# Gated mix of attention and a channel MLP: weight fetches, gate and row-max pacing moved in a kernel bound by one matmul stream

## The chip, the cores and the metric

The kernel runs on one core of one Trainium2 chip. The metric is device time of one execution in microseconds (us). TensorE (PE) multiplies, VectorE (DVE), ScalarE (ACT) and GpSimd (POOL) do the rest, and SyncE (SP) issues most transfers.

## The reference

```python
B, S, D, H, F = 1, 2048, 448, 16, 1792          # Dh = 28
g = sigmoid((x * gate_w).sum(-1, keepdims=True))
qkv = (x @ wqkv) split into q, k, v of 16 heads
p = softmax(q @ k^T * Dh ** -0.5)                # 2048 x 2048 for each head
a = (p @ v, heads joined) @ wo
y = layernorm(x)
b = gelu(y @ w1 + b1) @ w2 + b2
out = g * a + (1 - g) * b
```

All inputs and the output are float32. The kernel keeps accuracy with a split: each operand is a rounded high part (`h`, written by ScalarE or VectorE in the type fp32r) and a low part (`l`, value minus high part), and a product is h·h + h·l + l·h.

## The kernel before, in words

Tokens are worked on in 4 chunks (`NC`) of 512 (`CH`), heads in 4 groups (`NG`) of 4, one head to each 32-row strip of TensorE's array. TensorE's order is written out by hand for the whole kernel. In the first stage a scheduler orders the other engines; from the MLP on their order is by hand too. Each engine, and SP's queue, works strictly in its order.

**Stage 1, q, k and v (`qk_tile`, `v_tile`).** For each chunk `c` there are 7 tiles `m` of q and k columns and 4 tiles of v. In chunk 0, `load_wqk(m)` fetches a tile of weights into `wraw` (L147, 2 buffers), ScalarE makes the high part, GpSimd the low part. Results are copied out of the 8 PSUM banks in turn and written to DRAM by SP (L183). Between the tiles stand the steps of LayerNorm: `stats_fetch` and `ln_stats` (row statistics from `xk`), `ln_rows` and `ln_turn` (mean and reciprocal deviation, turned by TensorE with `ident` and written to DRAM), `ln_load` (read back to all partitions), `ln_fetch` and `ln_apply` (normalised x, on GpSimd). The first MLP weights (`fetch_w1`, `split_w1`) end the stage.

**Stage 2, the MLP.** For each chunk, `mlp1(f)` makes 14 tiles of 128 hidden units with 11 matmuls each (L512), and `mlp2(c, i)` makes 4 tiles of 128 tokens with 42 matmuls each (L525, L526, L529). I call them first and second product. In chunk 0 the weights are fetched and split as the tiles go: `split_w1` high part on ScalarE (L101), low part on GpSimd (L102), `split_w2` high part on ScalarE, low part on VectorE (L111). GpSimd also makes the low part of each hidden tile (L517).

**Row maxima beside it.** Attention needs the maximum of each row of scores first. `RowMax` computes q·k again, one unit being a 128 x 512 block (L346) in a PSUM bank which VectorE reduces (L326 one bank, L328 two). There are 16 groups of 65 units, 1040 in all; a group closes with a last reduction (L362), a TensorE transpose, a copy (L315) and a write. In the MLP `Filler` spreads the first 476 (`MLP_MAX`) over the matmuls: after each matmul `filler.run(n)` adds `n` to a slot count, and when six units are due by the share of slots passed, six are issued into banks 2 to 7.

```python
due = self.first + (self.upto - self.first) * min(1, self.slot / self.slots) - self.done
```

Before, each matmul counts 1; pacing begins at tile `FS` = 4 of chunk 0. A matmul into a bank whose reduction is not done waits, and everything behind it on TensorE too.

**The gate.** After the last chunk's first products ScalarE takes an exponential of `zall` (L572), and VectorE makes `gate` and `ngate` of it (L573 to L575). They are used in the last quarter of attention.

**Stage 3, attention.** 256 steps of 128 keys, with four score units each. `scores` takes five units at a time: three products per unit (L466), exponentials by ScalarE (L471), up to three row-max units, and then the products with v (L708). `load_wo(g)` in the first steps fetches a quarter of the output weights into one of 2 buffers `ob` (L685), VectorE copies the high part (L686), GpSimd makes the low part (L687). They are used from the last head group on.

Of the kernel before, what the change touches and what calls it, by code (L numbers as in the profile page):

```python
# [15 lines left out]
P = 128  # L16
S = 2048
D = 448
# [15 lines left out]
FS = 4  # L34
LQ = 12
# [4 lines left out]
def kernel(ctx: ExitStack, tc: tile.TileContext, xt, wqk, wv, wo, xk, w1, b1, w2, b2,  # L40
# [26 lines left out]
    nc.sync.dma_start(ones, one_t)  # L67
# [29 lines left out]
    def split_w1(f):  # L97
        r = wraw.pop((1, f)).rearrange("p (t x) -> p t x", t=4)
        t = mw1.tile([P, 8, P], F32R, name=f"w1f{f}")
        w1h[f], w1l[f] = t[:, 0:4], t[:, 4:8]  # L100
        nc.scalar.activation(w1h[f], r, AF.Copy)  # L101
        nc.gpsimd.tensor_sub(w1l[f], r, w1h[f].bitcast(F32))  # L102
# [33 lines left out]
    with tc.tile_pool(name="qx", bufs=2) as qx, tc.tile_pool(name="qo", bufs=3) as qo, \  # L136
# [9 lines left out]
        def load_wqk(m):  # L146
            raw = qx.tile([P, 4, P], F32, name="wraw", bufs=2)  # L147
            nc.sync.dma_start(raw, wqk[m])
            wh[m] = qw.tile([P, 4, P], F32R, name=f"wh{m}")
            wl[m] = qw.tile([P, 4, P], F32R, name=f"wl{m}")  # L150
            nc.scalar.activation(wh[m], raw, AF.Copy)
            nc.gpsimd.tensor_sub(wl[m], raw, wh[m].bitcast(F32))
# [81 lines left out]
        for t in range(4):  # L234
            load_x(0, t)
        for c in range(NC):
            for m in range(NM):
                if c == 0:
                    if m + 1 < NM:
                        load_wqk(m + 1)  # L240
                    if m == 1:
                        for t, s in ((ident, ident_d), (sel, sel_d), (b1s, b1)):
                            nc.sync.dma_start(t, s)
# [18 lines left out]
                if c == 1 and m >= 3 or c == 2 and m < 2:  # L262
                    stats_fetch(m - 1 if c == 1 else m + 6)
                if c == 1 and m >= 5 or c == 2 and m < 4:
                    ln_stats(m - 3 if c == 1 else m + 4)
                if c == 2 and m == 1:
                    ln_load(0)
                if c == 2 and m in (2, 3, 5, 6):
                    ln_fetch(0, (2, 3, 5, 6).index(m))
                if c == 2 and m in (4, 5) or c == 3 and m in (0, 1):  # L270
                    ln_apply(0, m - 4 if c == 2 else m + 2)
# [4 lines left out]
                if c == 3 and m == 1:  # L276
                    stages += [lnr[:, 0], lnr[:, 1]]
                if c == 3 and m in (1, 2, 4):
                    fetch_w1(m // 2 if m < 4 else 2) if m > 1 else fetch_w1(0)
# [224 lines left out]
    def mlp1(f):  # L504
# [6 lines left out]
        for i, (a, b) in enumerate(ops):  # L511
            nc.tensor.matmul(ps, a, b, start=(i == 0), stop=(i == len(ops) - 1))  # L512
            filler.run(1)
# [5 lines left out]
    def mlp2(c, i):  # L519
# [4 lines left out]
        for f in range(NF):  # L524
            nc.tensor.matmul(a, hh[f][:, sl], w2h[f], start=(f == 0), stop=False)  # L525
            nc.tensor.matmul(a, hh[f][:, sl], w2l[f], start=False, stop=False)  # L526
            if not last:
                filler.run(2)
            nc.tensor.matmul(a, hl[f][:, sl], w2h[f], start=False, stop=(f == NF - 1))  # L529
            if not last:  # L530
                filler.run(1)
# [7 lines left out]
    with tc.manual_schedule(engines={E.SP, E.Pool, E.Activation, E.DVE}):  # L539
        for c in range(NC):  # L540
            for f in range(NF):
                if c == 0:
# [7 lines left out]
                    if f == FS:  # L550
                        filler.spread(nc.sync, MLP_MAX, (NC * NF - FS) * 23 - 3 * NF)
                mlp1(f)
                if c == 0:
                    if f + 2 < NF:
                        split_w1(f + 2)
# [5 lines left out]
            if c == NC - 1:  # L561
# [9 lines left out]

                nc.scalar.activation(gate, zall, AF.Exp, scale=-1.0)  # L572
                nc.vector.tensor_scalar_add(gate, gate, 1.0)  # L573
                nc.vector.reciprocal(gate, gate)
                nc.vector.tensor_scalar(ngate, gate, -1.0, 1.0, op0=OP.mult, op1=OP.add)  # L575
# [9 lines left out]
            for i in range(TPC):  # L585
                mlp2(c, i)
                if c + 1 < NC and i < 3:
# [95 lines left out]
    def load_wo(g):  # L683
        worw = ao.tile([P, D], F32, name="ob")
        nc.sync.dma_start(worw, wo[:, g])  # L685
        nc.vector.tensor_copy(woh[:, g], worw)  # L686
        nc.gpsimd.tensor_sub(wol[:, g], worw, woh[:, g].bitcast(F32))  # L687
# [25 lines left out]
    with tc.manual_schedule(engines={E.SP, E.Pool, E.Activation, E.DVE}):  # L713
# [5 lines left out]
        for u in range(0, 4 * steps, U):  # L719
            units = list(range(u, min(u + U, 4 * steps)))  # L720
            while at < units[-1] // 4:
# [3 lines left out]
                if n == 0:  # L725
# [3 lines left out]
                    if 2 <= k < 6:  # L729
                        load_wo(k - 2)  # L730
# [88 lines left out]
```

## Time and profile before

| | us |
|---|---|
| median of 3 runs | 1157.71 (1154.74 to 1160.45) |
| profiled execution, time | 1159.02 |
| profiled execution, span of the core | 1157.2 |
| TensorE busy | 1127.3 |
| VectorE busy | 734.4 |
| ScalarE busy | 634.7 |
| GpSimd busy | 334.2 |

Times within the profile count from the start of the span. A line `L512` is line 512 of the kernel before. The mean granted TensorE clock of the execution is 0.988. In the busy rows a matmul's bar lasts longer than the distance to the next one, since matmuls are pipelined: what a matmul costs is read from start to start. Where the profile names who ended a wait for several signals, it names the one that came last.

### The profile page before, as it was taken

What the parts mean: (1) busy time and instruction counts of PE and PEld (TensorE: products, weight loads), DVE (VectorE), ACT (ScalarE), POOL (GpSimd) and SP (SyncE); (2) the same over time, 40 slices, a digit from 0 to 9 for tenths busy, and PEclk for the clock granted to TensorE, in tenths of its full rate; (3) what the DMA queues carried; (4) which work ended last, traced back from release to release, by engine and by line L of the source; (5) the groups of instructions that cost most, each with busy time, mean ns of one, the idle gap of its engine ahead of it and who ended that gap; (6) DMA issues with size and microseconds to landing.
All of it is one profiled execution on the core that took longest, in us unless ns stands there. A gap on an engine that the chain in (4) does not pass through costs nothing.

```text
span 1157.2 us, 19820 instructions
## 1 busy us (share of the span) xinstructions
PE 1127.3 (97%) x8136; PEld 681.4 (59%) x8136; DVE 734.4 (63%) x1031; ACT 634.7 (55%) x668; POOL 334.2 (29%) x355
## 2 busy tenths in 40 slices
PE   6999999999999999979999999999999999999998
PEld 4888667777767766834444444444444444454556
DVE  3443298888888987356666766676666766656102
ACT  5333550241131132157887878787887877756463
POOL 4033563343333341021223121310223024425050
PEclk9999999999999998989999999999999999999899
DMA  8888542010110105072101211112021003011101
GB/s 264 255 259 295 171 126 79 17 45 26 61 49 18 42 9 126 17 178 69 29 12 35 57 52 24 35 28 50 19 63 35 18 19 90 12 47 53 57 27 48
DMA packets 53519, 84.35 MB, mean 73 GB/s; under 512 B 8676, under 2 KB 28660, under 8 KB 52628
## 3 DMA queue, kind: packets, MB, share of 16 engines
q1 hardware_dynamic: 49236, 76.96, 22.0%
q0 software_dynamic: 4192, 6.12, 2.1%
q8 instruction: 64, 1.05, 0.4%
q14 instruction: 27, 0.22, 0.1%
HBM read 56.40 MB, written 26.49 MB: 72 GB/s over the span
## 4 chain that ended last, share of the span: by engine, by line
PE 89%; DVE 4%; DMA 2%; issue 2%; POOL 1%; ACT 1%; SPq 0%; DVEq 0%; POOLq 0%
PE bank L708 21%; PE bank L466 20%; PE bank L346 15%; PE bank L512 10%; PE bank L179 6%; PE bank L529 4%; PE bank L525 4%; PE bank L526 4%; DVE mx L328 3%; PE bank L195 2%; PE bank L618 1%; PE bank L619 1%; PE bank L620 1%; DMA lt<-ob 1%; DMA wraw<-in_wqk 0%
## 5 line engine op out<-in xcount | busy, mean ns | idle before, releaser
L471 ACT ACTIVATE pt<-bank 128x1536 f32<-128x1536 f32 (+1 forms) x408 | 482.4, 1234 | 166.7 <-PE bank L466 166.7
L326 DVE TENSOR_REDUCE mx<-bank 128x1 f32<-128x512 f32 x624 | 412.9, 686 | 167.6 <-PE bank L346 153.8
L708 PE MATMUL bank<-pt,vg 128*32 128x512 f32 x2038 | 263.5, 607 | 0.0
L328 DVE TENSOR_REDUCE mx<-bank 128x2 f32<-128x1024 f32 x200 | 234.8, 1217 | 32.9 <-PE bank L346 32.9
L346 PE MATMUL bank<-khi,qd 28*128 28x512 f32 x512 | 241.8, 480 | 1.9 <-DVE mx L326 1.9
L346 PEld LDWEIGHTS bank<-khi,qd 28*128 28x128 f32 x512 | 92.4, 181 | 150.1 <-DVE mx L326 109.5
L466 PE MATMUL bank<-qh,klo 28*128 28x512 f32 x1024 | 180.0, 397 | 0.0
L466 PE MATMUL bank<-qh,khi 29*128 29x512 f32 x768 | 162.1, 484 | 0.0
L512 PE MATMUL bank<-y,w1f 128*128 128x512 f32 x616 | 153.5, 399 | 3.0 <-POOL w1f L102 2.6
L512 PEld LDWEIGHTS bank<-y,w1f 128*128 128x128 f32 x616 | 112.2, 188 | 39.9 <-issue 11.3
L466 PE MATMUL bank<-ql,khi 28*128 28x512 f32 x768 | 134.4, 394 | 0.0
L517 POOL TENSOR_TENSOR hl<-h,hh 128x512 fp32r<-128x512 f32 x56 | 73.3, 1309 | 136.2 <-ACT h L516 95.4
L346 PE MATMUL bank<-khr,qd 28*128 28x512 f32 x512 | 86.5, 473 | 10.7 <-DMA ql<-qk 5.8
L708 PEld LDWEIGHTS bank<-pt,vg 128*32 128x32 f32 x2038 | 45.7, 108 | 84.6 <-issue 83.7
L466 PEld LDWEIGHTS bank<-qh,klo 28*128 28x128 f32 x1024 | 91.0, 187 | 4.3
L515 ACT ACTIVATE hh<-bank,b1s 128x512 fp32r<-128x512 f32 x56 | 38.6, 689 | 99.6 <-PE bank L512 99.6
L634 POOL DMA_DIRECT2D lt<-ob x15 | 10.9, 724 | 277.6 <-DVE ob L633 277.6
L535 ACT ACTIVATE h<-bank 128x448 f32<-128x448 f32 x16 | 8.7, 546 | 149.1 <-PE bank L529 113.8
L529 PE MATMUL bank<-w2h,hl 128*128 128x448 f32 x224 | 85.7, 383 | 0.0
L525 PE MATMUL bank<-w2h,hh 128*128 128x448 f32 x224 | 84.8, 379 | 0.0
L466 PEld LDWEIGHTS bank<-qh,khi 29*128 29x128 f32 x768 | 63.4, 183 | 36.0 <-ACT pt L471 31.8
L526 PE MATMUL bank<-w2l,hh 128*128 128x448 f32 x224 | 82.9, 370 | 0.0
(110 smaller groups left out, 1256.6 us busy)
## 6 DMA issues: line engine op xcount, KB each, us to landing
qk<-hl SPq DMA_DIRECT2D x28, 512.0 KB
xraw<-in_xt SPq DMA_DIRECT2D x16, 256.0 KB
vs<-vt SPq DMA_DIRECT2D x16, 256.0 KB
s<-in_xt SPq DMA_DIRECT2D x16, 256.0 KB
rc<-rls POOLq DMA_DIRECT2D x60, 64.0 KB, 2.2
bxr<-in_xk SPq DMA_DIRECT2D x8, 448.0 KB
gbs<-h SPq DMA_DIRECT2D x16, 224.0 KB
klo<-qk SPq DMA_DIRECT2D x16, 224.0 KB
```

Source lines behind the costliest of these rows:

```text
L179: nc.tensor.matmul(ps, a, b, start=(i == 0), stop=(i == len(ops) - 1))
L326: nc.vector.reduce_max(self.mx[:, c0:c0 + 1], bank[:, b0], axis=AX)
L328: nc.vector.reduce_max(self.mx[:, c0:c1 + 1:c1 - c0], bank[:, b0:b1 + 1], axis=AX)
L346: nc.tensor.matmul(bank[:, b], self.qds[self.n][r, i * P:(i + 1) * P], khi[self.n // NC][r, k * 512:(k + 1) * 512], start=True, stop=True)
L466: nc.tensor.matmul(bank[:, u % U], a[r, k * P:(k + 1) * P], b[r], start=(i == 0), stop=(i == 2))
L471: nc.scalar.activation(t, bank[:, b:b + len(units)], AF.Exp, scale=SCALE)
L512: nc.tensor.matmul(ps, a, b, start=(i == 0), stop=(i == len(ops) - 1))
L517: nc.gpsimd.tensor_sub(hl[f], h, hh[f].bitcast(F32))
L525: nc.tensor.matmul(a, hh[f][:, sl], w2h[f], start=(f == 0), stop=False)
L526: nc.tensor.matmul(a, hh[f][:, sl], w2l[f], start=False, stop=False)
L529: nc.tensor.matmul(a, hl[f][:, sl], w2h[f], start=False, stop=(f == NF - 1))
L708: nc.tensor.matmul(pv[32 * j:32 * j + 32, :], vg[n // NC][:, k, 32 * j:32 * j + 32], probs.pop(4 * step + j), start=(k == 0), stop=(k == N ...
```

## The change

- The tiles `wraw` get 4 buffers instead of 2, and weights are fetched two tiles ahead instead of one. The constants `ident`, `sel`, `b1s` and the write of `ones` move from the start to chunk 1. The LayerNorm steps stand at other tiles.
- The low parts of w1 tiles 0 to 5 are made by VectorE instead of GpSimd.
- A slot of the row-max pacing counts 0.233 for a first-product matmul (0.8 of that in chunk 0) and 0.205 for a second-product matmul, instead of 1. The total of slots changes with it.
- VectorE's three gate operations stand after the first tile of the last chunk's second product.
- Output weights are fetched in two pairs at steps 2 and 7, and split at steps 7 and 12, instead of one at each of steps 2 to 5, fetch and split together.

```diff
+W1, W2 = 0.233, 0.205
-    nc.sync.dma_start(ones, one_t)
...
-    def split_w1(f):
+    def split_w1(f, lo):
...
-        nc.gpsimd.tensor_sub(w1l[f], r, w1h[f].bitcast(F32))
+        lo.tensor_sub(w1l[f], r, w1h[f].bitcast(F32))
...
-            raw = qx.tile([P, 4, P], F32, name="wraw", bufs=2)
+            raw = qx.tile([P, 4, P], F32, name="wraw", bufs=4)
...
+        load_wqk(1)
...
-                    if m + 1 < NM:
-                        load_wqk(m + 1)
+                    if m + 2 < NM:
+                        load_wqk(m + 2)
...
-                if c == 0 and m in (3, 5):
-                    stats_fetch(m // 4)
-                if c == 1 and m in (1, 2):
-                    ln_stats(m - 1)
-                if c == 1 and m == 3:
+                if c == 1 and m >= 2 or c == 2 and m < 3:
+                    ln_stats(m - 2 if c == 1 else m + 5)
+                if c == 1 or c == 2 and m == 0:
+                    stats_fetch(m if c == 1 else 7)
+                if c == 1 and m == 1:
+                    for t, d in ((ident, ident_d), (sel, sel_d), (b1s, b1), (ones, one_t)):
+                        nc.sync.dma_start(t, d)
+                if c == 1 and m == 4:
                     ln_rows(0, TPC)
-                if c == 1 and m == 6:
+                if c == 2 and m == 0:
                     ln_turn(0, TPC)
...
-                if c == 2 and m == 1:
+                if c == 2 and m == 2:
                     ln_load(0)
...
-                    split_w1(m - 4)
+                    split_w1(m - 4, nc.vector)
...
-            filler.run(1)
+            filler.run(W1 if c else 0.8 * W1)
...
-                filler.run(2)
+                filler.run(2 * W2)
...
-                filler.run(1)
+                filler.run(W2)
...
-                        filler.spread(nc.sync, MLP_MAX, (NC * NF - FS) * 23 - 3 * NF)
+                        filler.spread(nc.sync, MLP_MAX, 11 * W1 * (0.8 * (NF - FS) + 3 * NF) + 3 * W2 * NF * (NT - 1))
...
-                        split_w1(f + 2)
+                        split_w1(f + 2, nc.vector if f < FS else nc.gpsimd)
...
                 nc.scalar.activation(gate, zall, AF.Exp, scale=-1.0)
-                nc.vector.tensor_scalar_add(gate, gate, 1.0)
-                nc.vector.reciprocal(gate, gate)
-                nc.vector.tensor_scalar(ngate, gate, -1.0, 1.0, op0=OP.mult, op1=OP.add)
...
                 mlp2(c, i)
+                if c == NC - 1 and i == 0:
+                    nc.vector.tensor_scalar_add(gate, gate, 1.0)
+                    nc.vector.reciprocal(gate, gate)
+                    nc.vector.tensor_scalar(ngate, gate, -1.0, 1.0, op0=OP.mult, op1=OP.add)
...
-    def load_wo(g):
-        worw = ao.tile([P, D], F32, name="ob")
-        nc.sync.dma_start(worw, wo[:, g])
-        nc.vector.tensor_copy(woh[:, g], worw)
-        nc.gpsimd.tensor_sub(wol[:, g], worw, woh[:, g].bitcast(F32))
+    worw = {}
+
+    def fetch_wo(g):
+        worw[g] = ao.tile([P, D], F32, name="ob")
+        nc.sync.dma_start(worw[g], wo[:, g])
+
+    def split_wo(g):
+        r = worw.pop(g)
+        nc.vector.tensor_copy(woh[:, g], r)
+        nc.gpsimd.tensor_sub(wol[:, g], r, woh[:, g].bitcast(F32))
...
-                    if 2 <= k < 6:
-                        load_wo(k - 2)
+                    if k in (7, 12):
+                        for i in range(2):
+                            split_wo(i if k == 7 else i + 2)
+                    if k in (2, 7):
+                        for i in range(2):
+                            fetch_wo(i if k == 2 else i + 2)
```

More of the change, by code (lines that the diff above doesn't have):

```diff
@@ L253 @@
                 qk_tile(c, m)
[L254 to L258 removed]
+                if c == 1 and m >= 2 or c == 2 and m < 3:
[6 more added lines that the diff above has]
+                if c == 1 and m == 4:
                     ln_rows(0, TPC)
[L260 removed]
+                if c == 2 and m == 0:
                     ln_turn(0, TPC)
[L262 to L265, printed above, removed]
[L266 to L271 removed]
+                if c == 2 and m == 2:
+                    ln_load(0)
+                if c == 2 and m in (3, 4, 6) or c == 3 and m == 0:
+                    if c == 2 and m == 6:
+                        ln_apply(0, 1)
+                    ln_fetch(0, {3: 0, 4: 1, 6: 2, 0: 3}[m])
+                if c == 2 and m == 5 or c == 3 and m in (1, 2):
+                    ln_apply(0, 0 if c == 2 else m + 1)
                 if c == 2 and m == 6:
@@ L275 @@
                     ln_turn(TPC, NT)
-                if c == 3 and m == 1:
-                    stages += [lnr[:, 0], lnr[:, 1]]
                 if c == 3 and m in (1, 2, 4):
-                    fetch_w1(m // 2 if m < 4 else 2) if m > 1 else fetch_w1(0)
+                    if m == 2:
+                        stages += [lnr[:, 0], lnr[:, 1]]
+                    fetch_w1(m // 2)
                 if c == 3 and m in (4, 5):
-                    split_w1(m - 4)
+                    split_w1(m - 4, nc.vector)
             for i in range(TPC):
@@ L502, with mlp1 @@
         hl[f] = mh.tile([P, CH], F32R, name=f"hl{f}")
-    def mlp1(f):
+    def mlp1(c, f):
         ps = bank[:, f % 2]
```

4 lines of the change are left out of this document (1 added, 3 removed).

## The prediction

> **What bounds the kernel now.** I read the page first: busy shares, the granted-clock row, and the chain that ended last.
>
> ```profile
> PE 1127.3 (97%) x8136; PEld 681.4 (59%) x8136; DVE 734.4 (63%) x1031; ACT 634.7 (55%) x668; POOL 334.2 (29%) x355
> ...
> PEclk9999999999999998989999999999999999999899
> ...
> PE 89%; DVE 4%; DMA 2%; issue 2%; POOL 1%; ACT 1%; SPq 0%; DVEq 0%; POOLq 0%
> ```
>
> TensorE is busy 97% of the span and carries 89% of the chain. It runs one instruction stream in order, so whatever delays a matmul anywhere delays the end. The change adds no matmul and takes none away: both programs hold the same 7110 TensorE instructions, and from the attention part on in the same order. Only the time in which TensorE waits, or runs at a lower clock, can change. The clock row has a few slices below 9, so next I asked for busy time by stretch around them.
>
> ```profile
> 29.95:33.36 3.41, 3.41 (x10) 2.75 (x9) 0.13 (x2) 0.66 (x2) 0.00 (x0) 0.50 0.81 209
> ...
> 446.40:449.75 3.35, 1.81 (x8) 0.77 (x7) 3.31 (x5) 0.00 (x0) 0.00 (x0) 1.00 0.92 201
> 449.80:456.60 6.80, 6.29 (x17) 5.09 (x17) 3.85 (x4) 0.00 (x0) 0.00 (x0) 0.50 0.75 188
> ...
> 497.60:507.80 10.20, 8.93 (x51) 3.93 (x52) 5.75 (x10) 2.37 (x2) 5.66 (x7) 0.50 0.64 176
> ```
>
> Columns: stretch, length, then busy time and count of PE, PEld, DVE, ACT, POOL, then granted clock, DMA share, GB/s. Each time TensorE had stood still for about half of some 3.4 us (1.81 busy of 3.35 before 449.8), the clock was 0.50 for a multiple of 3.4 us. A wait is thus paid twice: once as idle time, then as half speed.
>
> The Trainium skill ("TensorE: Matmul & The Clock Gate", What's actually happening) says that the clock falls after at least one idle window of about 3.4 us, and that these windows run freely. The trace agrees on the length but is stricter: a window that was half busy was enough. By the page's wording alone only the wait before 497.6 would have cost clock, and the sum below would be 5.1 us smaller (half of 3.41 and of 6.80); the rows decide.
>
> Last, the same view cut at the eight MLP sections (first and second product of each of four token chunks), with row-max units mixed in:
>
> ```profile
> 122.54:171.53 48.99, 44.73 (x197) 30.36 (x196) 32.52 (x32) 30.23 (x52) 34.80 (x25) 1.00 0.44 134
> 171.53:219.22 47.69, 46.29 (x241) 35.27 (x240) 43.06 (x46) 6.02 (x11) 16.58 (x13) 1.00 0.16 53
> 219.22:263.06 43.84, 43.84 (x215) 31.10 (x214) 37.07 (x39) 17.02 (x27) 16.74 (x13) 1.00 0.14 36
> 263.06:309.05 45.99, 45.65 (x241) 35.09 (x240) 40.19 (x43) 5.09 (x9) 16.55 (x13) 1.00 0.13 44
> 309.05:353.22 44.17, 44.17 (x216) 31.34 (x215) 37.16 (x39) 17.01 (x27) 16.38 (x13) 1.00 0.14 44
> 353.22:398.85 45.63, 45.63 (x241) 35.05 (x240) 40.18 (x44) 5.09 (x9) 16.88 (x14) 1.00 0.11 33
> 398.85:443.17 44.32, 44.32 (x216) 31.43 (x214) 37.35 (x38) 17.01 (x27) 16.41 (x13) 1.00 0.06 19
> 443.17:491.30 48.13, 45.93 (x222) 36.38 (x220) 22.62 (x27) 6.77 (x9) 1.61 (x2) 0.93 0.31 78
> ```
>
> The reader is to see that equal matmul work takes 43.8 to 49.0 us in one kind of section and 45.6 to 48.1 in the other.
>
> **Part 1: q, k weights in four buffers, constants later.** The first 33 us of the timeline:
>
> ```profile
> 1.17 0.42 SPq L67 DMA_DIRECT2D ones<-one_t  x1
> ...
> 21.87 0.40 SPq L148 DMA_DIRECT2D wraw<-in_wqk  x1
> 27.03 0.63 ACT L151 ACTIVATE wh<-wraw 128x512 fp32r<-128x512 f32 x1 [0.21 <-DMA wraw<-in_wqk]
> ...
> 21.33 0.50 PE L179 MATMUL bank<-xh,wl 128*128 128x512 f32 x1 [0.63 <-POOL wl L152]
> ...
> 25.57 0.39 PE L179 MATMUL bank<-xh,wh 128*128 128x512 f32 x1
> 25.80 0.39 PE L179 MATMUL bank<-xh,wl 128*128 128x512 f32 x1
> 27.71 0.50 PE L179 MATMUL bank<-xh,wh 128*128 128x512 f32 x1 [1.53 <-ACT wh L151]
> 28.06 0.39 PE L179 MATMUL bank<-xl,wh 128*128 128x512 f32 x1
> 29.09 0.51 PE L179 MATMUL bank<-xh,wl 128*128 128x512 f32 x1 [0.64 <-POOL wl L152]
> ```
>
> The bracket at a row's end gives the idle time before it and what ended it. A matmul follows the last after 0.23 us (25.57, 25.80). 27.71 comes 1.91 after its forerunner and 29.09 comes 1.03 after 28.06: 1.68 + 0.80 lost, and with 0.80 at 21.33, whose 0.63 us of idle time is the same, 3.3 us. The half clock at 29.95 to 33.36 costs 3.41 / 2 = 1.7. The cause stands in the SP row: the seventh weight is issued only at 21.87, behind a result write, and used 5.2 us later. With four buffers the order of the built program puts weights 0 to 3 and all of the first x ahead of any result write, and 4 to 6 behind only the low parts of 0 to 2; at 1.3 us each I work out that GpSimd has done those by about 13, so even at 5.2 us a transfer the last weight is there at about 18, and TensorE wants it at about 24. The `ones` write (0.42 on SP) leaves its place ahead of the first x tile, for which TensorE waits at the start. 3.3 + 1.7 + 0.4 = 5.4. From below 3.3, if the clock falls all the same; from above 6.0, with some smaller waits of the same kind. I take 5.4. Identity, selection rows, biases and `ones`, four issues on SP, now stand in chunk 1, some 30 us ahead of the first that needs one. The LayerNorm steps move with it: statistics are fetched in chunk 1 instead of 0, the row broadcast is read one tile later, and the w1 low parts 0 and 1 stand on VectorE ahead of result copies of chunk 3, so a late w1 tile would hold these, and SP's result writes behind them. GpSimd's last LayerNorm step ended at 94.9 (next row set); I work out about 97 now, and TensorE needs it when the MLP starts, then at about 117. Eight PSUM banks let result copies lag seven tiles (17 us). Nothing, unless that cover of 20 us is used up.
>
> **Part 2: MLP pacing and w1 low parts.**
>
> ```profile
> 93.57 1.29 POOL L133 TENSOR_TENSOR y<-s,y 64x512 fp32r<-64x512 f32 x1 [0.74 <-ACT y L129]
> ...
> 127.86 1.27 POOL L102 TENSOR_TENSOR w1f<-lnr,w1f 128x512 fp32r<-128x512 f32 x1
> 129.18 5.74 PE L512 MATMUL bank<-y,w1f 128*128 128x512 f32 x22 [1.01 <-POOL w1f L102]
> ...
> 146.33 3.47 DVE L328 TENSOR_REDUCE mx<-bank 128x2 f32<-128x1024 f32 x3
> 153.98 0.60 DVE L111 TENSOR_TENSOR w2l<-s,w2h 128x448 fp32r<-128x448 f32 x1
> 189.67 0.22 DVE L362 TENSOR_REDUCE mf<-mx 128x16 f32<-128x64 f32 x1
> ...
> 457.99 0.36 PE L529 MATMUL bank<-w2h,hl 128*128 128x448 f32 x1
> ...
> 460.42 0.36 PE L529 MATMUL bank<-w2h,hl 128*128 128x448 f32 x1
> ```
>
> First-product matmuls cost 0.23 us, second-product ones (460.42 - 457.99) / 12 = 0.2025. Section 219.22 has 154 of the first and 60 row-max units without a wait: 43.84 - 35.4 = 8.4, so six units cost 0.84. Taking 35.4 or 34.0 and the units (42, 72, 60, 72, 60, 72, 60, 38) off each section leaves 7.7, 3.6, 0, 1.9, 0.3, 1.5, 0.5 and, less 1.6 for early score products, 7.2: together 22.7 us of waiting.
>
> In the first section TensorE waits for w1 low parts (129.18: 1.0 us, from GpSimd L102): each f takes GpSimd two operations of about 1.3 (rows 93.57 and 127.86 are of that kind) where TensorE needs 11 x 0.23 = 2.5, and waits come on top. On VectorE (estimated from the w2 row at 153.98: 0.60 x 512 / 448 = 0.7, beside that 0.6) the parts 2 to 5 fit; from 6 on GpSimd has them again, against 2.5 plus the row-max units' share, 0.84 x 11 / 17.4 = 0.5, so one late tile at the hand-over stays.
>
> The rest is pacing. Six units need three reductions, 3.42 us of VectorE (3.47 less overlap). Before, 1154 slots / 476 units give six per 14.5 matmuls: 4.2 us in a first product, where chunk 0 also has 1.3 w2 parts (0.9): 4.3 wanted, too much; 3.8 in a second product, little above 3.42 plus some 0.5 where a group of 65 closes (the 0.22 at 189.67 and a copy like it). Now slots carry weights near these matmul times: 257.3 / 476 x 6 = 3.24, that is 17.4 matmuls in chunk 0's first product (4.84 us against 4.45 wanted), 13.9 in the others (4.04), 15.8 in second products (4.04). I leave 2.0 in the first section, 1.0 in the next, 0.6 in five and 0.5 in the last: 6.5. Gain 16.2; from below 8, if waits merely move to the sections that got denser, from above 22.7.
>
> **Part 3: the gate** is in the last section's 7.2:
>
> ```profile
> 446.19 0.17 DVE L573 TENSOR_SCALAR gate<-gate 128x16 f32<-128x16 f32 x1 [2.96 <-ACT gate L572]
> 448.05 0.50 PE L346 MATMUL bank<-khr,qd 28*128 28x512 f32 x2 [0.84 <-DVE mx L328]
> ...
> 484.20 1.60 PE bank L466 x12
> ```
>
> VectorE stood 2.96 us for ScalarE's exponential with reductions queued behind, and TensorE for banks; then 6.8 us at half clock. After the first tile's second product (12 us later) the exponential is long done. These are counted above; three operations of 0.2 us stay.
>
> **Part 4: output weights in pairs, split later.**
>
> ```profile
> 497.82 0.39 DVE L686 CAST woh<-ob 128x448 fp32r<-128x448 f32 x1 [23.88 <-DMA ob<-in_wo]
> 498.87 0.79 PE L346 MATMUL bank<-khr,qd 28*128 28x512 f32 x1 [5.81 <-DMA ql<-qk]
> ...
> 492.41 2.37 ACT L471 ACTIVATE pt<-bank 128x1536 f32<-128x1536 f32 x2 [0.32 <-PE bank L466]
> 510.54 2.37 ACT L471 ACTIVATE pt<-bank 128x1536 f32<-128x1536 f32 x2 [0.30 <-PE bank L466]
> 522.26 2.36 ACT L471 ACTIVATE pt<-bank 128x1536 f32<-128x1536 f32 x2 [0.35 <-PE bank L466]
> ```
>
> VectorE takes the first copy while its transfer is under way, 23.88 us idle; row-max reductions queue behind and TensorE stops for 5.81 us (the releaser named is a DMA, the banks were held by VectorE), then runs at half clock for 10.2. Four steps, each with a pair of exponentials, from 510.54 to 522.26 take 11.72, 2.93 a step. From 492.41 to 522.26 stand seven steps, 29.85 against 20.5: 9.3 lost. Now the first copies stand behind 15 reductions, five steps or 14.6 us on, while the transfer landed 5.4 us after 492.41: 9 us of cover. If it fails, VectorE blocks as before. The second pair is issued after GpSimd split the first, at about 17, lands at about 22 and is wanted at 26. What is next late: nothing I see; two copies at once (0.8) just about fit VectorE's 0.8 us of slack a step. I take 9.0, from below 4 (second pair 5 us late), from above 9.3.
>
> **Sum.** 5.4 + 16.2 + 9.0 = 30.6. The profiled execution took 1159.0 (span 1157.2 and 1.8 around it), 1.3 above the median of 1157.7. 1159.0 - 30.6 = 1128.4, and from the median 1127.1: I say 1128.
>
> **The rivals.**
> *MLP waits move.* The denser first products leave VectorE as short of time as before; only the low parts and the gate are won, 8 us. For: 4.04 leaves 0.1 over 3.42 + 0.5 at a closing. Against: 3.8, below that sum, cost no more than 1.5 to 1.9 us a section. 1159.0 - 5.4 - 8 - 9.0 = 1136.6.
> *Output weights still late.* SP's queue holds the second pair behind GpSimd; a 5 us slip blocks VectorE as at 497.82. For: SP waits for GpSimd there. Against: 4 us of cover. 1159.0 - 5.4 - 16.2 - 4 = 1133.4.
> *Weights not early.* The buffers are there but transfers share bandwidth and land no sooner. For: the DMA share at 30 us was 0.81. Against: the row at 21.87 shows a late issue, not a slow transfer. 1159.0 - 0.4 - 16.2 - 9.0 = 1133.4.
> *Slower: the clock falls in first products.* If two bank waits fall in one 3.4 us stretch, as at 446 to 450, that event costs 3.35 - 1.81 = 1.5 idle and 3.4 of clock, 4.9. Seven events outweigh the gain. With one for every second group of six in three first products (18 events) it is 1128 + 88 = 1216. For it speaks the 0.1 us margin; against, that waits of 0.1 us are far from half a window. It decides once waits pass 0.8 us a group.
>
> **How the numbers follow.** The forecast 0.74, MLP waits move 0.12, output weights late 0.05, weights not early 0.06, the clock 0.03. The range: all upper bounds, 6.0 + 22.7 + 9.3, off the median give 1120; the lower bounds of the first two parts with 8 of the third, 3.3 + 8 + 8, off the profiled time give 1140; between them lie the three middle rivals, and what is left out is the fourth and several lower bounds at once. A measurement of this kernel tells about 0.5% (5.8 us) from no change. Faster by more 0.95, within 0.02 (several lower ends at once), slower 0.03.
>
> **What would show it.** Right: no gap over 0.3 us on TensorE between 20 and 33 us, full clock there, at 450 and at 498; VectorE without a wait for the output weights; first section near 43, no section over 47. Wrong: any new stretch at half clock before 1060, or VectorE idle for a DMA after 480.

## The result and the profile after

The changed kernel takes 1137.76 us (median of four runs, 1136.69 to 1140.50) against 1157.48 (1154.74 to 1160.45) for the kernel before: a ratio of 0.983, with a 95% interval of 0.980 to 0.986. It is faster by 1.7%, 19.7 us by the medians. The prediction said 1128, a gain of 30.6; about two thirds of that came. The profiled execution took 1136.69, with a span of 1134.9 against 1157.2, and the accounts below are made on the spans, where 22.3 us went. The page of the changed kernel, with the rows that answer to those of before:

```profile
PE 1114.4 (98%) x8136; PEld 675.8 (60%) x8136; DVE 739.6 (65%) x1037; ACT 634.6 (56%) x668; POOL 323.8 (29%) x349
...
PEclk9999999999999999999999999999999999999999
...
PE 90%; DMA 3%; DVE 2%; POOL 2%; issue 1%; ACT 1%; SPq 1%; POOLq 0%; ACTq 0%
```

TensorE is still what bounds the kernel. The clock row has no slice below 9 left, but slices of 28 us hide stretches of 3.4. The view by stretch, cut at the waits that remain and at the half clock behind them (length, then busy time and count of PE, PEld, DVE, ACT, POOL, then granted clock, DMA share, GB/s):

```profile
64.27:67.10 2.83, 0.40 (x2) 0.00 (x0) 0.71 (x2) 1.40 (x3) 0.00 (x0) 1.00 0.84 307
68.52:71.93 3.41, 3.41 (x9) 2.67 (x9) 1.53 (x6) 0.79 (x2) 0.00 (x0) 0.50 0.82 111
467.47:469.79 2.32, 0.49 (x3) 0.18 (x3) 2.32 (x4) 0.52 (x1) 0.00 (x0) 1.00 0.27 99
471.29:474.70 3.41, 3.41 (x13) 2.62 (x16) 0.00 (x0) 0.00 (x0) 0.00 (x0) 0.50 0.00 0
1051.56:1054.97 3.41, 3.41 (x17) 0.60 (x16) 0.00 (x0) 1.95 (x2) 0.00 (x0) 0.50 0.04 10
```

The stretches at half clock at 30, 450 and 498 us are gone, 20.5 us long together. Two new ones have come, each behind a wait that was not there before: 68.5 (for x) and 471.3 (for a bank). The one near 1050 us is the old one at 1071, half as long. The same view at the eight MLP sections (first and second product of each chunk in turn):

```profile
120.99:167.65 46.66, 42.84 (x192) 29.61 (x191) 34.55 (x33) 30.12 (x52) 28.58 (x21) 1.00 0.51 159
167.65:211.29 43.64, 43.54 (x230) 34.12 (x228) 38.16 (x40) 6.13 (x11) 16.59 (x13) 1.00 0.20 58
211.29:256.96 45.67, 45.67 (x228) 31.68 (x226) 39.43 (x44) 17.59 (x28) 16.72 (x13) 1.00 0.11 34
256.96:300.15 43.19, 43.19 (x231) 34.22 (x229) 36.85 (x38) 4.52 (x9) 16.56 (x13) 1.00 0.13 41
300.15:345.31 45.16, 45.16 (x221) 31.66 (x220) 38.92 (x43) 17.02 (x27) 16.70 (x13) 1.00 0.17 48
345.31:389.38 44.07, 44.07 (x236) 34.37 (x234) 37.16 (x38) 5.09 (x9) 16.56 (x13) 1.00 0.10 34
389.38:434.60 45.22, 45.22 (x221) 31.82 (x220) 39.06 (x44) 17.02 (x27) 16.71 (x13) 1.00 0.08 23
434.60:481.52 46.92, 44.99 (x234) 35.66 (x232) 31.75 (x34) 6.77 (x9) 3.56 (x5) 0.96 0.31 82
```

In the six middle sections TensorE now waits 0.1 us in all by length less busy time, where it was 1.7 before. (Bars overlap, so this counts only waits longer than the overlap; the prediction's way, each matmul and unit at its price, counts more, and is used further down.) The first and the last are the ones that stay long: 3.8 us of waits in the first, 1.9 in the last and half clock after that.

The account by stage, in us. The MLP begins at 120.99 instead of 122.54 and lasts 360.53 instead of 368.6; from its end to the ninth step of attention it takes 21.1 instead of 31.2; the rest, to the last exponentials, takes 614.2 instead of 617.0. Row numbers such as L691 count lines in the kernel of the run that is named.

| Stage | forecast | profile |
|---|---|---|
| start, to the first MLP product | 5.4 | 1.6 |
| MLP with w1 parts and gate | 16.2 | 8.0 |
| first steps of attention | 9.0 | 10.0 |
| rest of attention | 0 | 2.8 |
| sum | 30.6 | 22.4 |

### The profile page after: what moved, and what is told of

Its sections match the earlier page's. It is cut to its first block, busy times and chain, and to the rows that moved or that the text cites. A ratio compares the mean times of both kernels' runs of the same rounds, so it can differ in the third digit from the quotient of the medians.

```text
span 1134.9 us, 19822 instructions
## 1 busy us (share of the span) xinstructions
PE 1114.4 (98%) x8136; PEld 675.8 (60%) x8136; DVE 739.6 (65%) x1037; ACT 634.6 (56%) x668; POOL 323.8 (29%) x349
## 3 DMA queue, kind: packets, MB, share of 16 engines
q8 instruction: 64, 1.05, 0.4%
## 4 chain that ended last, share of the span: by engine, by line
PE 90%; DMA 3%; DVE 2%; POOL 2%; issue 1%; ACT 1%; SPq 1%; POOLq 0%; ACTq 0%
PE bank L713 22%; PE bank L466 20%; PE bank L346 15%; PE bank L512 11%; PE bank L179 5%; PE bank L529 4%; PE bank L525 4%; PE bank L526 4%; DMA xraw<-in_xt 2%; PE bank L195 2%; PE bank L618 1%; PE bank L619 1%; PE bank L620 1%; POOL w1f L102 1%; DVE mx L328 1%
## 5 line engine op out<-in xcount | busy, mean ns | idle before, releaser
L466 PE MATMUL bank<-qh,klo 28*128 28x512 f32 x1024 | 177.4, 393 | 0.0
L346 PE MATMUL bank<-khr,qd 28*128 28x512 f32 x512 | 81.0, 466 | 0.2
```

The source lines that it names most:

```text
L346: nc.tensor.matmul(bank[:, b], self.qds[self.n][r, i * P:(i + 1) * P], khi[self.n // NC][r, k * 512:(k + 1) * 512], start=True, stop=True)
L466: nc.tensor.matmul(bank[:, u % U], a[r, k * P:(k + 1) * P], b[r], start=(i == 0), stop=(i == 2))
```

## The experiments

All ratios below are to the kernel before on the same chip. Runs of one program differ by some us (the first kernel below took 1140.09 to 1149.52), and each has one profile. In the profiles TensorE's first matmul comes anywhere from 5.2 to 6.5 us, and a half clock comes or does not. So I read the stage that an edit touches, and the times only beside that.

**Each part of the change undone, on the changed kernel.** First the output weights.

```diff
-                    if k in (7, 12): ...
-                    if k in (2, 7): ...
+                    if 2 <= k < 6:
+                        load_wo(k - 2)
```

> The changed kernel with the output weights as before: one fetch and split a step at steps 2 to 5. Theory (the pairs and the later split are worth what the start of attention gained, 10.0 us): the first eight steps take about 37 us again instead of 27, VectorE idles over 20 us for a transfer, a half-clock stretch of some 10 us follows, and the span is 1145. Rival (VectorE was late for the weights because the gate and the row maxima had made everything late, and that is mended by the other parts): the steps stay near 27 to 31 us, span 1135 to 1139.

Measured: 1145.71 us, ratio 0.990 (0.985 to 0.995). The timeline, and the stretch at half clock behind:

```profile
488.99 0.39 DVE L686 CAST woh<-ob 128x448 fp32r<-128x448 f32 x1 [17.09 <-DMA ob<-in_wo]
...
490.04 0.79 PE L346 MATMUL bank<-khr,qd 28*128 28x512 f32 x1 [5.56 <-DMA ql<-qk]
```

```profile
488.37:498.61 10.24, 8.57 (x47) 3.67 (x50) 5.49 (x10) 2.36 (x2) 5.64 (x7) 0.50 0.65 178
```

The first eight steps take 36.7 us instead of 27.0. VectorE waits 17 us in its queue for the transfer, TensorE 5.6, and half clock follows. With the other parts in place this one is worth 9.7 us in the profiles; by the two ratios, 0.990 and 0.983, it is some 8 us.

Next the first stage, as before but with w1 parts 0 and 1 left on VectorE.

```diff
-            raw = qx.tile([P, 4, P], F32, name="wraw", bufs=4)
+            raw = qx.tile([P, 4, P], F32, name="wraw", bufs=2)
... (load_wqk one ahead; constants, stats_fetch, ln_* in their old places)
```

> The changed kernel with its first stage as before: two weight buffers, constants at the start, LayerNorm fetches and steps in their old places (low parts 0 and 1 of w1 stay on VectorE). Theory (the start gained 5.4 us, but the statistics' fetches now crowd the third x chunk and give 4 back there): the MLP begins 1.5 us later, at 122.5; the gaps at 21, 27.7 and 29 us are back, the one at 64 to 67 us is gone; span 1136.5. Rival (the stall at 64 us has another cause than the moved fetches, it stays): the MLP begins at 126 to 127, span 1140 to 1141.

Measured: 1140.06 us, ratio 0.985 (0.981 to 0.989); the MLP begins at 121.62. Two rows of the timeline, and the stretch where the stall was:

```profile
20.58 0.50 PE L180 MATMUL bank<-xh,wh 128*128 128x512 f32 x1 [1.38 <-ACT wh L152]
...
28.02 0.50 PE L180 MATMUL bank<-xh,wh 128*128 128x512 f32 x1 [1.21 <-ACT wh L152]
```

```profile
60.00:72.00 12.00, 12.00 (x58) 10.60 (x58) 5.47 (x18) 3.13 (x7) 0.00 (x0) 1.00 0.94 291
```

The old gaps return and the stall at 64 us is gone: both belong to this part, and nearly cancel (121.62 against 120.99). The span, 1140.1, missed the expected 1136.5, because in this profile a wait of 1.44 us in the first MLP section fell so that the clock dropped behind it (that section 49.2, 2.6 longer), and the half clock near 1055 us lasted 6.8 us instead of 3.4.

Then the pacing of row maxima.

```diff
-            filler.run(W1 if c else 0.8 * W1)
+            filler.run(1)
... (2 and 1 in the second product, 1154 slots)
```

> The changed kernel with the old pacing of row maxima in the MLP (every matmul one slot, 1154 slots). Theory (the pacing gained 3 to 4 us in the middle sections and gave as much back by the stall at the last token tile, since the last section now holds 50 units instead of 38): the six middle sections take 3.5 us more together, the last has no stall and no half clock at 467 to 475 and takes about 43 us for its 38 units instead of 46.9 for 50; span 1135 to 1136, so the pacing as it stands is worth nearly nothing. Rival (the pacing is worth most of the 8 us won in the MLP): span 1140 or more.

Measured: 1140.52 us, ratio 0.986 (0.982 to 0.990). The last section:

```profile
441.45:484.20 42.75, 42.55 (x221) 34.12 (x220) 22.53 (x27) 6.77 (x9) 3.89 (x6) 1.00 0.38 93
```

No stall there, 42.75 us for 38 units. The six middle sections take 271.8, as in the kernel before (271.6), against 267.0 in the changed kernel. The whole MLP takes 362.0 against 360.5: the pacing as it stands is worth 1.5 us, 4.9 won in the middle, 0.8 in the first, and 4.2 lost in the last section. Part of that is only units that stand elsewhere, at 0.14 us each: six fewer in the first section, six fewer in the middle, twelve more in the last. Without them the pacing won nothing in the first section and 4.0 in the middle, and lost 2.5 in the last, by the stall. By the time alone the rival would be nearer; but the span of 1138.9 holds a stall for x of 3.5 us at 68 us and a half clock of 6.8 us near 1052, which this edit does not touch. The same run prices two other edits against the kernel before, whose pacing it shares: the last section, 47.9 there, is 5.2 shorter, for which the later gate is the only edit that touches that section, and the first, 49.0 there, is 1.5 shorter (47.45), which I put down to the w1 low parts. No run undid the gate by itself.

Last, the w1 low parts.

```diff
-                        split_w1(f + 2, nc.vector if f < FS else nc.gpsimd)
+                        split_w1(f + 2, nc.gpsimd)
... (tiles 0 and 1 too)
```

> The changed kernel with all low parts of w1 on GpSimd as before. Theory (VectorE needs 1.4 us for each beside GpSimd's work, so moving six of them won little): the first section, 46.7 us, takes 0 to 2 us more; span 1135 to 1137. Rival (each of the four low parts moved in the section saves GpSimd's 1.3 us, and TensorE the wait): the first section takes 4 to 5 us more; span 1139 to 1140.

Measured: 1140.71 us, ratio 0.987 (0.982 to 0.991); the first section takes 50.87. Its timeline at the start of that section:

```profile
122.84 0.73 PE L512 MATMUL bank<-y,w1f 128*128 128x512 f32 x2 [1.15 <-ACT w1f L101]
124.90 6.71 PE L512 MATMUL bank<-y,w1f 128*128 128x512 f32 x22 [1.32 <-POOL w1f L102]
132.97 4.29 PE L512 MATMUL bank<-y,w1f 128*128 128x512 f32 x16 [1.36 <-POOL w1f L102]
```

4.2 us more, which is the rival's figure but not its way: the waits are 2.5 longer together than in this section of the changed kernel, and half clock from 124.5 costs 1.7. The first of the three waits is for ScalarE's high part, and so not the edit's alone: the MLP began at 116.50 here, with no stall at 64 us, though up to 90 us this is the changed kernel. (Against the next kernel below, whose MLP began as early and whose first section took 46.96, it is 3.9 us more.) So that stall is a close thing. In six profiles of kernels with this first stage it was 2.4, 2.2, 3.5, 2.6, 1.3 and 0 us.

**The three waits that are left, each taken away by itself.** The x loads of the third chunk, issued earlier:

```diff
                 qk_tile(c, m)
+                if c == 1 and m >= 3:
+                    load_x(2, m - 3)
...
-                if c + 1 < NC:
+                if c != 1 and c + 1 < NC:
                     load_x(c + 1, i)
```

> The changed kernel with the four loads of the third x chunk issued after tiles 3 to 6 of the second chunk's products, ahead of that tile's statistics fetch, instead of behind all of them. Theory (the stall at 64 to 67 us is x that was asked for behind six statistics fetches on a busy DMA): TensorE has no gap over 0.5 us between 60 and 75 us and runs at full clock there, the MLP begins 3 to 4.3 us earlier, at 116.5 to 118; span 1131 if nothing is late next, 1133 if the first w1 tiles then are. Rival (the transfers' rate is the limit, not their order): the stall stays or moves to 70 to 100 us, MLP begins at 120 to 122, span 1134 to 1137.

Measured: 1133.53 us, ratio 0.981 (0.978 to 0.983). SP's queue in the changed kernel, and then the earlier loads and the stretch where the stall was:

```profile
54.30 0.46 SPq L165 DMA_DIRECT2D xraw<-in_xt  x1
57.13 0.47 SPq L165 DMA_DIRECT2D xraw<-in_xt  x1
...
59.94 1.17 SPq L165 DMA_DIRECT2D xraw<-in_xt  x1
...
65.70 0.63 ACT L166 ACTIVATE xh<-xraw 128x512 fp32r<-128x512 f32 x1 [2.11 <-DMA xraw<-in_xt]
67.10 0.50 PE L179 MATMUL bank<-xh,wh 128*128 128x512 f32 x1 [2.44 <-DVE xh L170]
```

```profile
39.75 0.57 SPq L165 DMA_DIRECT2D xraw<-in_xt  x1
49.18 0.50 SPq L165 DMA_DIRECT2D xraw<-in_xt  x1
53.83 0.57 SPq L165 DMA_DIRECT2D xraw<-in_xt  x1
...
60.00:75.00 15.00, 15.00 (x69) 12.39 (x69) 8.22 (x22) 6.48 (x13) 0.00 (x0) 1.00 0.92 316
```

The last three of the four loads are issued 6 to 15 us earlier, and there is no stall, full clock, and the MLP begins at 116.38. One profile without a stall would say little here, since the run just above had none either; but none of the six profiles of kernels with the earlier loads has one, against five of six without. With its cause gone the start gains 6.2 us on the kernel before, of which 1.1 is the earlier first matmul of this profile. So 5.1 came where 5.0 was forecast without the 0.4 for the first matmul. In the changed kernel it is 1.6, less 0.4 for its first matmul: 3.9 were given back at the third chunk.

Row maxima that end earlier:

```diff
-... + 3 * W2 * NF * (NT - 1))
+... + 3 * W2 * NF * (NT - 1) - 4)
```

> The changed kernel with 4 slots fewer in the sum over which the MLP's row maxima are spread (253.3 instead of 257.3), so that the last of them are issued some 5 us before the last token tile. Theory (the stall of 1.8 us at 467 to 470 and the half clock behind it come from bank 7, which the last units still hold when the last tile's product wants it): stall and half clock go, the last section takes 43.5 with 48 to 50 units instead of 46.9; span 1131.5. Rival (VectorE is simply behind by then, since groups come denser): the wait moves to the units before, the last section stays at 46 to 47; span 1135.

Measured: 1134.92 us, ratio 0.982 (0.980 to 0.984). The end of the row maxima in the changed kernel, and the last section of this one:

```profile
465.62 0.73 PE L346 MATMUL bank<-khr,qd 28*128 28x512 f32 x6
...
467.46 0.50 PE L346 MATMUL bank<-khr,qd 28*128 28x512 f32 x2
...
469.05 1.88 DVE L326 TENSOR_REDUCE mx<-bank 128x1 f32<-128x512 f32 x3
469.79 0.47 PE L525 MATMUL bank<-w2h,hh 128*128 128x448 f32 x1 [1.82 <-DVE mx L326]
```

```profile
435.77:478.48 42.71, 42.71 (x228) 34.32 (x226) 28.05 (x31) 6.77 (x9) 3.57 (x5) 1.00 0.34 90
```

Eight units were issued from 465.62 on, VectorE needed to 469.7 for the one in bank 7, and the last token tile is accumulated in bank 7. With the units earlier the wait and the half clock go and the MLP takes 357.75 instead of 360.53. The span, 1133.3 and not 1131.5, has the stall for x and a half clock of 6.8 us at 1048 instead of 3.4.

The w1 split ahead of the product:

```diff
+                if c == 0 and f + 2 < NF:
+                    split_w1(f + 2, nc.vector if f < FS else nc.gpsimd)
                 mlp1(c, f)
                 if c == 0:
-                    if f + 2 < NF:
-                        split_w1(f + 2, nc.vector if f < FS else nc.gpsimd)
```

> The changed kernel with w1 tile f + 2 split ahead of the first product f instead of behind it, so that the high and low parts stand ahead of the two activations of f on ScalarE and ahead of the low part of h on GpSimd and VectorE. Theory (the waits for low parts in the first section are a chain: end of f, two activations, high part, low part of h, low part of w1, about 4.2 us, not a lack of engine time): six waits of 0.3 to 1.0 us go, the first section takes 42 to 44 us instead of 46.7; span 1131 to 1132. Rival (GpSimd and VectorE are too slow in sum, 1.3 to 1.6 us for each operation beside the other): the waits stay with some changed places, 46 to 47 us.

Measured: 1134.20 us, ratio 0.982 (0.980 to 0.983). Its timeline in the first section, and two stretches there:

```profile
139.86 0.50 PE L346 MATMUL bank<-khr,qd 28*128 28x512 f32 x2 [0.56 <-DVE mx L328]
140.99 0.50 PE L346 MATMUL bank<-khr,qd 28*128 28x512 f32 x2 [0.63 <-DVE mx L328]
```

```profile
138.24:141.65 3.41, 2.22 (x10) 0.97 (x9) 3.41 (x5) 2.52 (x6) 3.41 (x4) 1.00 0.47 147
141.65:145.06 3.41, 3.41 (x9) 2.62 (x9) 3.41 (x3) 0.43 (x1) 2.73 (x2) 0.50 0.62 183
```

All waits for low parts are gone (two of 0.24 and 0.35 us for ScalarE have come), so they were a chain and not a lack of engine time. But the section still takes 46.14: TensorE now comes to the row-max units earlier than VectorE has reduced the last ones, and two waits of 0.6 us in one window brought half clock. My 42 to 44 left out what is late next.

**Together, and further.** The three edits in one kernel:

> The three edits together: x of the third chunk earlier, row maxima ending earlier, w1 split ahead of the product. Theory (they are separate waits): MLP begins at 116.5 to 118, its first section 42 to 44, its last 43.5; sum of gains 4 + 3.4 + 3.5 = about 11, span 1124, a time of 1126 and a ratio of 0.973. Rival (the earlier MLP meets w1 tiles that are not there yet): the first section is 45 or more, span 1128 to 1131.

Measured: 1129.87 us, ratio 0.979 (0.976 to 0.981), span 1126.4. The MLP begins at 116.71, its first section takes 44.02, its last 42.70; they are separate waits. The sum is 8.5, not 11, since four waits of 0.6 us for VectorE in the first two sections remain. Four more kernels follow it. With the low parts of tiles 2 to 5 back on GpSimd:

> The kernel with the three edits, with the low parts of w1 tiles 2 to 5 back on GpSimd. Theory (with the split ahead of the product the chain is short enough on either engine; the move to VectorE only won time because the split stood behind): first section within 0.5 us of 44.0, span 1126 to 1127. Rival (GpSimd, 2.6 to 2.9 us a tile against 2.5 us on TensorE until row maxima begin, falls behind): one or two waits for low parts of 0.5 to 1 us, first section 45 to 46.

Measured: 1128.66 us, ratio 0.978 (0.976 to 0.979), first section 44.08: with the split ahead, the move of these four to VectorE is worth nothing. This is the lowest ratio of all that ran, 2.2% under the kernel before, though its interval overlaps those of its neighbours. With fewer row maxima in the first section:

> The kernel with the three edits, and the first product of chunk 0 given 0.6 instead of 0.8 of the other products' weight, in the running and in the sum of slots. Theory (what is left in the first section is VectorE late with reductions, four waits of 0.6 us, since it also has the low parts of w1 and w2, slowed beside GpSimd): the waits go, the first section takes 2 us less beyond the units that leave it, the others take up 9 units at 0.14 us each and no wait; span 1124 to 1125. Rival (the later sections then come denser than VectorE can reduce): waits of 0.6 us there, span 1126 to 1127.

Measured: 1131.06 us, ratio 0.978 (0.975 to 0.981): the rival's way. The first section takes 42.98, the second 47.93 with three waits of 0.6 us and half clock; the span is 1131.1, above the rival's 1127. With an earlier end of the row maxima in attention:

> The kernel with the three edits (x earlier, row maxima ending earlier, w1 split ahead), and in attention the row maxima spread over 3 slots fewer, without the last closing unit. Theory (the last stall of the trace, 0.95 and 1.04 us behind VectorE near 1040 us and the half clock after it, is two units and the closing one issued back to back because one slot was lost to rounding): both waits go and the clock stays full to the end, 3.7 us less where the half clock lasted 3.4 us; span 1122 to 1123. Rival (the units meet VectorE's queue wherever they stand): a wait of about 1 us stays some us earlier, span 1125 to 1126.

Measured: 1130.84 us, ratio 0.980 (0.977 to 0.982); the stall stands as it did:

```profile
1042.26 0.50 PE L348 MATMUL bank<-khi,qd 28*128 28x512 f32 x1 [0.95 <-DVE mx L328]
1043.79 0.28 PE L314 MATMUL bank<-ident,mf 128*16 128x128 f32 x1 [1.04 <-DVE mf L364]
```

My reason was wrong: no slot is lost, but at most three units run in a step, every step has three, and fewer slots change nothing. So, on the kernel with the low parts on GpSimd and with this edit, 484 units before attention instead of 476:

> The kernel with the three edits (x earlier, row maxima ending earlier, w1 split ahead of the product) with w1 low parts from tile 2 on GpSimd, 484 instead of 476 row-max units before attention, and the rest spread over 3 slots fewer without the last closing unit. In the kernel that had only the last of these, the stall near 1040 us stayed: at most three units run in a step, 564 in 188 steps fill every one, and nothing can be caught up. Theory (with 8 units fewer to do the last unit stands two steps ahead of the closing one): the waits of 0.95 and 1.04 us and the half clock of 3.4 to 6.8 us after them (1.7 to 3.4 lost) go, the MLP takes 1 us more for 8 units and attention 1 less; span 1122 to 1124 against 1127.1 without it, ratio to the kernel before about 0.974. Rival (the denser row maxima in the MLP cost waits there): MLP 359 or more instead of 356, span 1125 to 1127.

Measured: 1131.79 us, ratio 0.981 (0.978 to 0.983). Near 1040 us there is no wait and no half clock, and attention from its ninth step to the last exponentials takes 609.2 us instead of 615.6. The MLP takes 359.4 instead of 355.9, as the rival had it. And something came that neither had: the last output has landed at 1122.9 and the program ends at 1130.0.

```profile
1030.00:1060.00 30.00, 30.00 (x225) 17.71 (x221) 5.12 (x9) 15.69 (x14) 13.84 (x12) 1.00 0.09 32
1120.60:1122.90 2.30, 0.00 (x0) 0.00 (x0) 0.71 (x2) 0.00 (x0) 0.00 (x0) 1.00 0.96 359
1122.90:1130.00 7.10, 0.00 (x0) 0.00 (x0) 0.00 (x0) 0.00 (x0) 0.00 (x0) 0.53 0.00 0
```

In every other kernel that stretch is 1.3 us. The trace has GpSimd's closing drain instruction at 10.97 us instead of 1.42, and the other engines wait for it. Why is open; no run was made on it.

## Why the prediction was right or wrong, step by step

**Right: what bounds, and that waits are paid twice.** TensorE's count of matmuls stayed (8136 records in both pages), and its busy time fell from 1127.3 to 1114.4 us. Half clock lasted 27.3 us before (without the end of the program) and 10.2 after; at half speed that is at most 8.5 of the 22.4 us. Of the signs that the prediction named for itself, the full clock at 30, 450 and 498 us and the copies without a wait came true; the first section near 43 us did not, it took 46.66.

**Part 4, output weights: right.** 9.0 forecast, 10.0 in the profile, 9.7 undone.

```profile
482.83 2.37 ACT L471 ACTIVATE pt<-bank 128x1536 f32<-128x1536 f32 x2 [0.32 <-PE bank L466]
...
492.40 0.69 DVE L691 CAST woh<-ob 128x448 fp32r<-128x448 f32 x2
...
502.64 2.37 ACT L471 ACTIVATE pt<-bank 128x1536 f32<-128x1536 f32 x2 [0.33 <-PE bank L466]
```

The copies stand at 492.40 with no wait, and seven steps from 482.83 take 19.8 us, not 29.9. The rival "output weights still late" falls, and the gain is 0.7 above the upper end of 9.3 that was stated.

**Part 1, the start: the mechanism right, the term 3.8 too large.** TensorE has no gap between 20 and 33 us and full clock, as forecast, so the rival "weights not early" falls. But 1.6 is below the lower end of 3.3 that was stated. What failed is the sentence on the LayerNorm steps, "Nothing, unless that cover of 20 us is used up". I asked when TensorE needs normalised x, and not what stands behind the moved fetches in SP's queue: the x loads of the third chunk. How little room the transfers have there stands in the kernel before, a DMA share of 0.96:

```profile
60.00:68.00 8.00, 8.00 (x41) 7.34 (x40) 5.22 (x16) 2.43 (x6) 0.00 (x0) 1.00 0.96 342
```

The wait of 2.44 us and half clock of 3.4 gave most of the gain back, and it is the "new stretch at half clock" that the prediction named as its sign of being wrong (the one at 471 us is another). GpSimd's last LayerNorm step ended near 105 us, not 97; a w1 fetch in SP's queue waited for it (issued at 105.08), TensorE did not.

**Parts 2 and 3, the MLP: 16.2 mis-sized, 8.0 came.** Counted as the prediction counted it (35.4 or 34.0 us and 0.14 a unit taken off each section), the waiting fell from 22.7 to 14.7 us. The first section keeps 6.2 where I left 2.0, the last 4.3 where I left 0.5; the six between keep 4.1, where I left 4.0. So two terms were too large, by 4.2 and 3.8, and they make up the 8.2 that are missing.

*The first section.* The low parts on VectorE were sized at 0.7 us, from one row that stood beside nothing. The twelve operations of that line (L111) in the first section before took 0.60 to 1.71 us, and I took one of the shortest. The changed kernel:

```profile
125.77 1.29 POOL L517 TENSOR_TENSOR hl<-h,hh 128x512 fp32r<-128x512 f32 x1 [20.73 <-ACT h L516]
126.19 1.42 DVE L102 TENSOR_TENSOR w1f<-lnr,w1f 128x512 fp32r<-128x512 f32 x1 [2.94 <-ACT w1f L101]
127.66 5.28 PE L512 MATMUL bank<-y,w1f 128*128 128x512 f32 x22 [0.72 <-DVE w1f L102]
...
154.01 0.73 PE L512 MATMUL bank<-y,w1f 128*128 128x512 f32 x2 [0.99 <-POOL w1f L102]
```

Beside GpSimd's low part of h it took 1.4. But that is the smaller share: of 3.8 us of idle time in the section, 1.05 are two waits for VectorE's parts, and 2.7 are five waits for GpSimd's, from tile 6 on, where I had left one late tile. I had taken the waits for a lack of GpSimd time; the split moved ahead of the product took all of them away, with tiles 2 to 5 on either engine, so they came from the place of the split in the engines' order: the split for tile f + 2 stood behind the gelu and the low part of tile f, which wait for its product.

*The last section.* The pacing did in the middle sections what was forecast, and the last section lost most of it again. I had left 0.5 us there; it was 1.82 of idle time and 1.7 of clock at the hand-over to the last token tile. The step that I overlooked is the total of slots. The old total, 1154, is 48 less than the matmuls that are counted: 52 tiles of 11 and 15 token tiles of 42 make 1202. So the old pacing was done some 10 us early; in the changed kernel with the old pacing the last units were issued at 463.57, and the last token tile began at 474.04. The new total, 257.3, is just what the weighted matmuls add up to, so the last units are issued at 467.46 and not yet reduced when that tile wants bank 7 at 467.97. The exact total also puts twelve more units into the last section.

*The gate* did what was said: 5.2 us by the last section of two kernels with the same pacing, and VectorE reached its operations at 448.88 with no wait.

**The rest of attention, 2.8 us that I had not forecast:** 1.7 is half clock near 1051 us, 3.4 us long instead of 6.8. Other kernels here have either length with the same two waits before it, so this is where the windows fell and no gain of the change. The other 1.1 I have not traced; in the other kernels with 6.8 us of half clock there this stretch took 615.6 to 616.8, so it is of the size of the scatter.

**The rivals.** "MLP waits move", 1136.6, is nearest in time to what was measured, and in part in mechanism: 8 us won in the MLP, a new wait in a section that got denser. Its sum is near too: low parts and gate won 6.7, the pacing 1.5. But the denser first products of the later chunks, where it put the trouble, have no wait. That its time fits the profiled 1136.69 is luck: the start came 3.8 us short of the forecast, and attention 3.8 us above it. The forecast had some of that luck: without the 2.8 us of attention that were not forecast the time would have been 1140.6, above the stated range of 1120 to 1140. The clock did not fall in first products of the later chunks.

## What to carry to other kernels

When transfers are moved, list what is queued behind them at the new place and the DMA's share there, not only who needs the moved data; when work is spread evenly over a stretch, end it early enough that the last pieces are worked off before the next user wants their buffers, and check that the total it is spread over is the count that really runs. Price an operation by a row that ran beside what it will run beside. And when a wait for a product is long, look at its place in the queues of the engines that make it before moving it to another engine: moving the split one statement up did what a second engine had not.

## What the runs showed of the hardware

**VectorE and GpSimd.** The 128x512 subtraction takes VectorE 0.69 us alone and 1.36 to 1.42 beside GpSimd, and it then ends 0.54 to 0.55 us after GpSimd's operation does (126.19 + 1.42 against 125.77 + 1.29). GpSimd's own takes 1.29 us alone and 1.66 where VectorE's began first (at 138.23 in the changed kernel, 0.3 us behind one on VectorE). A VectorE subtraction with one operand in PSUM is not touched, as the kernel before shows (GpSimd's 1.62 there comes from a VectorE subtraction with both inputs in SBUF, which ran until 87.01):

```profile
86.55 1.62 POOL L128 TENSOR_TENSOR s<-s,lnr 128x512 f32<-128x512 f32 x1
86.94 0.68 DVE L182 TENSOR_TENSOR hl<-bank,hl 128x512 fp32r<-128x512 f32 x1
```

The Trainium skill ("SBUF — State Buffer", Who interferes with whom) says that a VectorE instruction with two inputs in SBUF and a GpSimd one that reads SBUF take an exclusive lock, that the later one blocks for the whole of the other, and that VectorE with one SBUF input, outside its two-port modes, does not contend. The rows agree: VectorE's operation ends a fixed time after GpSimd's, as if held until then, and the one with its input in PSUM isn't held.

**The clock.** In 13 of the 14 profiles (the last kernel's has none before its end) all stretches at half clock after the first 20 us begin on a grid of 3.413 us in their own run, to 1 ns. Cutting each of the 13 on its grid, and leaving out the end of the program, by TensorE's busy share in a window at full clock: each of 27 windows below 0.58 was followed by half clock, none of those above 0.66 was, and of nine between them five were. So two waits of 0.6 us in one window can cost another 1.7, as at 138 us above, and much the same waits across two windows cost nothing: in the last kernel 0.52 and 0.63 us, 1.1 apart at 136.40 and 137.53, left both windows over 0.8 busy and the clock full. The prediction's "a window that was half busy was enough" did not go far enough.
